# Dense matmuls behind a block of values issued as two of 64 stationary columns

## The chip, the cores and the metric

The kernel runs on one core of a Trainium2 chip, as one program. The metric is the device time of one execution in microseconds (us). A core has TensorE (PE: matmuls, with the loads of their stationary operand recorded apart as PEld), VectorE (DVE), ScalarE (ACT), GpSimd (POOL) and SyncE (SP), which run side by side and wait for each other through semaphores.

## What is computed

Sigmoid attention over 8 batches, 12 heads, 448 tokens and a head dimension of 64, and behind it a two-layer block with a gated hidden layer:

```python
scores = scale * np.matmul(q, k.transpose(0, 1, 3, 2)) - np.log(S)
attn = 1.0 / (1.0 + np.exp(-scores))
attn_out = np.matmul(attn, v)                         # (8, 12, 448, 64)
x = np.ascontiguousarray(attn_out.transpose(0, 2, 1, 3)).reshape(B * S, H * D)   # (3584, 768)
h = x @ w_in                                          # w_in: 768 x 2048
g = h * (1.0 / (1.0 + np.exp(-beta * h)))
out = (g @ w_out)                                     # w_out: 2048 x 768, out: float32
```

## The kernel before

All matmul operands are float16, sums are float32 in eight PSUM banks of 128 x 512. A matmul has a stationary operand (rows x columns, loaded first) and a moving one that streams past it; `128*64` in the profile means 128 rows and 64 columns of stationary operand. A matmul that uses fewer rows or columns than 128 is put at a `tile_position` in the array, and such matmuls can run beside each other at different positions.

The work on TensorE is of four kinds.

**Scores** (`score`, line 229). Heads are taken in pairs ("slots"), two slots are a quad, 24 quads in all, three for each batch. A *visit* (`visit`) computes the scores of one quad for one block of keys: eight matmuls of 32*128 over 448 queries (blocks 0 to 2 of 128 keys), or, for the last block of 64 keys, eight or, two quads at once, sixteen of 32*64. The scores of a visit fill the four score banks, and one ScalarE instruction turns them into weights (`weigh_two`, line 257, 1792 elements in each of 128 partitions), held in `attns`.

**Values** (`attend`, line 332). Once all four key blocks of a quad have weights, sixteen matmuls sum weights times values: four of 64*64 for the last block, then twelve of 128*64 in pairs, one head at column 0 and the other at column 64. VectorE copies the two sums to `xTs` (line 341).

**First layer** (`blocks`, line 523): for two batches at a time, 168 matmuls of 128*128 in one run, in a seven-product scheme, with sixteen dense units between them. Three such runs lie at 128.70, 215.97 and 302.53 us. The first two batches take the plain `dense1` (line 354) instead.

**Dense units.** Everything else, from 42 us on mostly the second layer (`strassen`, line 643, also a seven-product scheme on sums of two hidden tiles; `single`, line 437; `dense2`, line 384). A unit is one matmul, 128*128 over 384 columns in the second layer and over 448 in `dense1`. The units stand in a list, `fill`, in a fixed order; the eight units of one product add up in one bank, which is held from the product's first unit until VectorE or ScalarE may take it out.

The order of TensorE's work is written by a planner that runs when the kernel is built. From 42 us on it goes through 74 visits (n = 0 to 73). After the score matmuls of visit n it sets

```python
todo = left_us(L1B) if g < 2 * QPB else left_us(len(fill)) - RESERVE[n >= max(turn_at)]
pace = (todo + phase["values"] * AV_US) / phase["visits"]
owed = pace + MORE.get(n, 0) * M2_US
```

where `left_us` is the cost of the units left, 0.164 us each in the second layer (`M2_US`) and 0.148 in `dense1`; `phase` counts the visits and the blocks of values that are left until the next run of first-layer blocks; and `MORE` is a table of corrections by visit. Then units are issued while half a unit's cost is below `owed`, each taking its cost off. The values of a quad become due in the next quad's first visit. They are issued in the first place where `spent`, the units already issued in this visit, is at least `LATE.get(n, 0)` (3 at visit 8, 10 at visits 68 and 72, and at seven others), and take `AV_US` off `owed`. In a quad's first visit (`jt` is 0) they also need `clear()`: fewer than two banks held by dense sums, or two held and the next unit opening none (a product's third and fourth group and the first half of its fifth count as opening). In later visits of the quad, units are issued until `clear()` holds. After the last visit, and before visits 33 and 54, `first_layer` issues values that are due, the rest of the units but eight, and the run of blocks, which itself takes sixteen units.

Of the kernel before, what the change touches and what calls it, by code (L numbers as in the profile page):

```python
# [13 lines left out]
def kernel(  # L14
# [10 lines left out]
    nc = tc.nc  # L25
# [3 lines left out]
    B, H, S, D = q.shape  # L29
# [109 lines left out]
    def last_base(s: int) -> int:  # L139
        return (s % 2 ^ swapped(s // 2)) * KL  # L140
# [76 lines left out]
    def score_tile():  # L217
        i, j = scored[n_sc[0] % len(scored)]
        n_sc[0] += 1
        width[i] = width[j] = S  # L220
        return ps[:, i : j + 1]

    def score(sco, u0: int, s: int, jt: int, hh: int, e: int, c0: int, n: int):
        g, lo = s // 2, (s % 2 * 2 + hh) * BLK
        assert (g, "k") in ready and all(
            (g, "q", c) in ready for c in range(c0 // BLK, (c0 + n) // BLK, NB // 2)
        )
        base, nk = (last_base(s), KL) if jt == JF else (0, P)
        nc.tensor.matmul(  # L229
            sco[base : base + nk, hh, u0 : u0 + n],  # L230
            kT[g][lo : lo + BLK, jt * P : jt * P + nk, e],
            qT[g][lo : lo + BLK, c0 : c0 + n, e],
            start=(e == 0),
            stop=(e == PAIR - 1),
            tile_position=(lo, base),
        )

    places = {}

    def weigh(sco, n: int):  # L240
# [28 lines left out]
        nc.scalar.copy(out=dummy, in_=attns[:, slot, 0, 0:1])  # L269

    def visit(g: int, jt: int, also=()):
        if jt < JF:
            todo = [[s] for s in (2 * g, 2 * g + 1)]
        else:
            todo = [[2 * h, 2 * h + 1] for h in (g, *also)]
        todo = [(score_tile(), slots) for slots in todo]
        for e in range(PAIR):
            for sco, slots in todo:
                for s in slots:
                    for hh in range(2):  # L280
                        score(sco, 0, s, jt, hh, e, 0, S)
        if len(todo) == 2 and len(scored) == 2:
            ats = weigh_two(ps[:, 0:4, 0:S], places.get(g, ()))
        else:
            ats = [weigh(sco, S) for sco, _ in todo]
        for slot, (_, slots) in zip(ats if n_sc[0] % 2 == 0 or len(todo) == 1 else ats[::-1], todo):
            for s in slots:
                at_use(slot, (s, jt, 0), slice(0, S))
        return ats[-1]


    def half_visit(g: int, c0: int, second: int):
        slots = (2 * g, 2 * g + 1)
        scos = [score_tile() for _ in slots]
        plan = [(s, jt, sco, jt * QH) for jt in (0, 1) for s, sco in zip(slots, scos)]
        widths = [S, S]
        if second:
            plan = [(s, 2, sco, 0) for s, sco in zip(slots, scos)]
            plan += [(s, JF, scos[0], QH) for s in slots]
            widths = [S, QH]  # L300
        for i in range(0, len(plan), 2):
            for e in range(PAIR):
                for s, jt, sco, u0 in plan[i : i + 2]:
                    for hh in range(2):
                        score(sco, u0, s, jt, hh, e, c0, QH)
        if len(scored) == 2 and not second:
            two = weigh_two(ps[:, 0:4, 0:S], ())
            ats = dict(zip(map(id, scos), two if n_sc[0] % 2 == 0 else two[::-1]))
        else:
            ats = {id(sco): weigh(sco, n) for sco, n in zip(scos, widths)}  # L310
        for s, jt, sco, u0 in plan:
            at_use(ats[id(sco)], (s, jt, c0), slice(u0, u0 + QH))

    def attend(g: int, c0: int, n: int, part=(0, 1)):
        b, t = divmod(g, QPB)
        if b not in xTs:
            xTs[b] = xTp.tile([P, NHC, S], FP16, tag="xT", name="xT")
        assert (b, "v") in ready and (b, "full", t, HQ - 1) in ready
        slots = [2 * g + x for x in part]
        avs = [bank() for _ in slots]  # L320
        todo = [(s, av, jt) for s, av in zip(slots, avs) for jt in range(JF)]
        rest = [(s, av, JF) for s, av in zip(slots, avs)]
        todo = rest + todo if n == S else todo + rest
        first, last = {}, {}
        for s, _, jt in todo:
            first.setdefault(s, jt)
            last[s] = jt
        for s, av, jt in todo:
            at = at_take((s, jt, c0))
            base, nk = (last_base(s), KL) if jt == JF else (0, P)  # L330
            for hh in range(2):
                nc.tensor.matmul(  # L332
                    av[hh * D : (hh + 1) * D, 0:n],
                    vs[b][base : base + nk, 2 * (s % NPAIR) + hh, jt],
                    at[base : base + nk, hh, 0:n],
                    start=(jt == first[s]),
                    stop=(jt == last[s]),
                    tile_position=(base, hh * D),
                )
        for s, av in zip(slots, avs):  # L340
            nc.vector.tensor_copy(out=xTs[b][:, s % NPAIR, c0 : c0 + n], in_=av[:, 0:n])  # L341
            ready.update((b, s % NPAIR, c) for c in range(c0, c0 + n, QH))
# [4 lines left out]
    def dense1(b: int, dc: int, hc: int, c0: int = 0, n: int = S):  # L347

        off = (b % 2) * S + c0
        assert all((b, hc, c) in ready for c in range(c0, c0 + n, QH))  # L350
        if hc == 0:
            m2s[b, dc] = bank(n, (b, dc))
        m1 = m2s[b, dc]
        nc.tensor.matmul(  # L354
            m1,
            w_in16[:, hc, dc * P : (dc + 1) * P],
            xTs[b][:, hc, c0 : c0 + n],
            start=(hc == 0),
            stop=(hc == NHC - 1),
        )  # L360
        if hc < NHC - 1:
            return
        release((b, dc))
        assert "beta" in ready
        sg = sigp.tile([P, S], FP32, tag="sg", name="sg")
        nc.scalar.activation(  # L366
            out=sg[:, 0:n], in_=m1, func=AF.Sigmoid, bias=0.0, scale=beta_sb[:, dc : dc + 1]
        )
        nc.vector.tensor_tensor(  # L369
            out=gt[:, dc, off : off + n], in0=m1, in1=sg[:, 0:n], op=ALU.mult  # L370
        )
# [7 lines left out]
    def dense2(t: int, half: int, dc: int):  # L379

        if dc == 0:
            m2s[t, half] = bank(HALF, (t, half))
        m2 = m2s[t, half]
        nc.tensor.matmul(  # L384
            m2,
            gt[:, dc, cols(t)],
            w_out16[:, dc, half * HALF : (half + 1) * HALF],
            start=(dc == 0),
            stop=(dc == NDC - 1),
        )  # L390
        if dc == NDC - 1:
            leave(t, half, m2)
# [25 lines left out]
    def single(t: int, n: int, dc: int, piece=None):  # L418

        if (n, dc) == (0, 0):  # L420
            if (t, 0) not in sums:
                sum_of_halves(t)
            for half in range(1 + (t < NT - 1)):
                m2s[t, 1 - half] = bank(HALF, (t, 1 - half))
        if piece is not None and (n, dc) == (1, 0):
            m2s[t, 0, piece] = bank(CUTS[piece + 1] - CUTS[piece], (t, 0, piece))
        both = sums[t, 0]
        half, x, w = (
            (1, hid(t, 0), B12),
            (0, hid(t, 1), B21),  # L430
            (1, both, B22),
            (0, both, B11),
        )[n]
        m2 = m2s[(t, half) if piece is None else (t, half, piece)]
        stop = n > 1 and dc == ND - 1
        w = w[:, dc] if piece is None else w[:, dc, CUTS[piece] : CUTS[piece + 1]]
        nc.tensor.matmul(m2, x[:, dc], w, start=(n < 2 and dc == 0), stop=stop)  # L437
        if stop:
            leave(t, half, m2, piece)

# [99 lines left out]

    def blocks(b: int, other, scores: int):

        kept = {}
        rest = sorted(used, key=used.get)
        firsts = [i for i in rest if width[i] == S and i not in held.values()][:2]
# [17 lines left out]
        for i in range(NB1 + 1):  # L563
            p5 = scratch(6 + i % 2, 1).bitcast(FP32)
            if i < NB1:
# [6 lines left out]
                D = take("D", i)  # L572
# [59 lines left out]
    def strassen(t: int, i: int, dc: int):  # L632

        name, x, _, op, w = product(t, i)
# [5 lines left out]
        if first:  # L640
            m2s[t, name] = bank(HALF, (t, name))
        m2 = m2s[t, name]
        nc.tensor.matmul(  # L643
            m2,
            (x if op is None else sums[t, i])[:, dc],
            w[:, dc],
            start=first,
            stop=(dc == ND - 1),
# [108 lines left out]
    with tc.manual_schedule():  # L757
# [28 lines left out]
        for r, (to, n) in parts.items():  # L786
            nc.sync.dma_start(
                out=to[:, 0 : n * D],
# [96 lines left out]
        def left_us(n: int):  # L885
            return sum(u[0] for u in fill[at_fill[0] : n])

        AV_US = 1.5
        GLANCE = 3
        MORE = {  # L890
# [31 lines left out]
        def values(g: int):  # L922
# [3 lines left out]
            attend(g, 0, S)  # L926
            owed -= AV_US
            phase["values"] -= 1
# [15 lines left out]
        for n, (g, jt, also) in enumerate(visits):  # L944
# [25 lines left out]
            todo = left_us(L1B) if g < 2 * QPB else left_us(len(fill)) - RESERVE[n >= max(turn_at)]  # L970
            pace = (todo + phase["values"] * AV_US) / phase["visits"]
            phase["visits"] -= 1
# [46 lines left out]
```

## Time and profile before

| | |
|---|---|
| time, median of 3 runs | 373.27 us (373.2 to 373.52) |
| span of the profiled execution, first to last instruction | 371.2 us |
| time outside that span, by the median | 2.1 us |
| PE busy | 365.5 us (98%), 2906 matmuls |
| ACT busy | 259.7 us (70%) |
| DVE busy | 254.4 us (69%) |
| POOL busy | 80.5 us (22%) |
| visits 0 to 32, 33 to 53, 54 to 73, from their first score to the blocks' start | 86.58, 52.75 and 52.02 us |

The profile shows one execution. Its times are single ones and are compared with the median by adding the time outside the span. A busy TensorE isn't one at its peak, since the ends of matmuls are modelled; starts are measured, and what follows is read from differences of starts. Lines of the timeline merge equal instructions that follow each other: the first number is the start of the first, the second the length of all.

### The profile page before, as it was taken

What the parts mean: (1) busy time and instruction counts of PE and PEld (TensorE: products, weight loads), DVE (VectorE), ACT (ScalarE), POOL (GpSimd) and SP (SyncE); (2) the same over time, 40 slices, a digit from 0 to 9 for tenths busy, and PEclk for the clock granted to TensorE, in tenths of its full rate; (3) what the DMA queues carried; (4) which work ended last, traced back from release to release, by engine and by line L of the source; (5) the groups of instructions that cost most, each with busy time, mean ns of one, the idle gap of its engine ahead of it and who ended that gap; (6) DMA issues with size and microseconds to landing.
All of it is one profiled execution on the core that took longest, in us unless ns stands there. A gap on an engine that the chain in (4) does not pass through costs nothing.

```text
span 371.2 us, 7295 instructions
## 1 busy us (share of the span) xinstructions
PE 365.5 (98%) x2906; PEld 184.6 (50%) x2906; DVE 254.4 (69%) x479; ACT 259.7 (70%) x311; POOL 80.5 (22%) x120
## 2 busy tenths in 40 slices
PE   8999999999999999999999999999999999999997
PEld 4566544443444455544444445554444455555665
DVE  4435796777496967787666667778767667679671
ACT  5995766798967668887877749887678647883000
POOL 7732431221131013233131003233100002230000
PEclk9999999999999999999999999999999999999999
DMA  9999999893368030029829410017803111000334
GB/s 173 195 197 204 202 205 206 193 123 51 51 86 174 1 87 1 2 49 130 171 37 212 106 25 20 3 29 110 171 2 85 44 44 42 1 2 1 87 85 129
DMA packets 36226, 34.65 MB, mean 93 GB/s; under 512 B 9424, under 2 KB 32608, under 8 KB 36192
## 3 DMA queue, kind: packets, MB, share of 16 engines
q0 software_dynamic: 30288, 22.47, 42.3%
q1 hardware_dynamic: 5904, 11.71, 11.1%
q8 instruction: 23, 0.38, 0.4%
q14 instruction: 11, 0.09, 0.1%
HBM read 45.62 MB, written 11.01 MB: 153 GB/s over the span
## 4 chain that ended last, share of the span: by engine, by line
PE 93%; ACT 5%; issue 1%; DVE 0%; ACTq 0%
PE ps L643 27%; PE ps L523 26%; PE ps L229 11%; PE ps L332 10%; PE ps L354 9%; PE ps L384 4%; PE ps L437 4%; ACT attns L242 3%; ACT attns L257 1%; PE ps L812 1%; ACT sg L366 1%; DVE gt L369 0%; ACT osb L664 0%; DVE still L806 0%; ACT osb L399 0%
## 5 line engine op out<-in xcount | busy, mean ns | idle before, releaser
L257 ACT ACTIVATE attns<-ps,nlogs 128x1792 f16<-128x1792 f32 x75 | 131.7, 1756 | 41.1 <-PE ps L229 41.0
L643 PEld LDWEIGHTS <-sum 128*128 128x128 f16 x440 | 40.5, 98 | 37.3 <-issue 12.5
L537 POOL TENSOR_TENSOR gt<-attns,sg 128x448 f16<-128x448 f32 x21 | 23.9, 1137 | 141.7 <-ACT sg L534 141.7
L229 PE MATMUL ps<-qT,kT 32*128 32x448 f16 (+3 forms) x864 | 52.3, 339 | 1.1 <-ACT attns L242 0.6
L534 ACT ACTIVATE sg<-ps,beta_sb 128x448 f32<-128x448 f32 x72 | 45.2, 632 | 8.4 <-PE ps L523 5.9
L523 PE MATMUL ps<-xT,w_in 128*128 128x448 f16 x216 | 49.2, 353 | 0.0
L523 PE MATMUL ps<-xT,w_S 128*128 128x448 f16 x216 | 49.2, 352 | 0.0
L643 PE MATMUL ps<-w_T,sum 128*128 128x384 f16 x264 | 48.7, 327 | 0.0
L537 DVE TENSOR_TENSOR gt<-ps,sg 128x448 f16<-128x448 f32 x72 | 44.2, 618 | 4.0 <-ACT sg L534 3.8
L341 DVE CAST xT<-ps 128x448 f16<-128x448 f32 (+1 forms) x54 | 28.8, 567 | 21.5 <-PE ps L332 21.5
L523 PEld LDWEIGHTS <-w_in 128*128 128x128 f16 x288 | 28.0, 98 | 26.6 <-issue 0.7
L661 DVE TENSOR_TENSOR osb<-ps,osb 128x384 f32<-128x384 f32 x55 | 30.5, 554 | 15.1 <-PE ps L643 12.8
L332 PE MATMUL ps<-attns,v 128*64 128x448 f16 (+3 forms) x432 | 40.4, 340 | 0.1
L354 PE MATMUL ps<-xT,w_in 128*128 128x448 f16 (+1 forms) x240 | 39.5, 316 | 0.6 <-DVE gt L369 0.6
L630 DVE TENSOR_TENSOR sum<-gt 128x1024 f16<-128x1024 f16 x55 | 36.5, 678 | 0.2
L369 DVE TENSOR_TENSOR gt<-ps,sg 128x448 f16<-128x448 f32 (+1 forms) x40 | 20.0, 527 | 22.4 <-ACT sg L366 22.3
L125 POOL DMA_DIRECT2D raw<-in_q_dram x26 | 14.4, 555 | 92.8 <-DVE kT L212 84.7
L643 PE MATMUL ps<-w_out,gt 128*128 128x384 f16 x176 | 33.3, 327 | 0.0
L643 PE MATMUL ps<-w_out,sum 128*128 128x384 f16 x176 | 32.3, 327 | 0.0
L583 DVE TENSOR_TENSOR ps<-ps,attns 128x448 f32<-128x448 f32 x24 | 15.2, 632 | 23.3 <-PE ps L523 19.4
L523 PEld LDWEIGHTS <-w_S 128*128 128x128 f16 x216 | 21.1, 98 | 19.4
L354 PEld LDWEIGHTS <-w_in 128*128 128x128 f16 x240 | 22.0, 98 | 16.9 <-issue 5.8
(52 smaller groups left out, 364.3 us busy)
## 6 DMA issues: line engine op xcount, KB each, us to landing
out_dram<-osb SPq DMA_DIRECT2D x100, 96.0 KB, 2.2
raw<-in_k_dram POOLq DMA_DIRECT2D x23, 224.0 KB, 5.3
raw<-in_q_dram POOLq DMA_DIRECT2D x21, 224.0 KB, 4.1
v<-in_v_dram POOLq DMA_DIRECT2D x16, 192.0 KB, 6.9
w_in<-in_moe_w_in_dram POOLq DMA_DIRECT2D x8, 384.0 KB, 11.9
w_out<-in_moe_w_out_dram POOLq DMA_DIRECT2D x4, 768.0 KB, 15.0
v<-in_v_dram POOLq DMA_DIRECT2D x16, 144.0 KB, 7.5
out_dram<-osb SPq DMA_DIRECT2D x5, 144.0 KB, 2.4
```

The source lines that it names most:

```text
L229: nc.tensor.matmul(sco[base : base + nk, hh, u0 : u0 + n], kT[g][lo : lo + BLK, jt * P : jt * P + nk, e], qT[g][lo : lo + BLK, c0 : c0 + n ...
L257: nc.scalar.activation(out=attns[:, slot : slot + 2].rearrange("p n h s -> p (n h) s"), in_=sco, func=AF.Sigmoid, bias=nlogs[:, 0:1], scal ...
L332: nc.tensor.matmul(av[hh * D : (hh + 1) * D, 0:n], vs[b][base : base + nk, 2 * (s % NPAIR) + hh, jt], at[base : base + nk, hh, 0:n], start ...
L341: nc.vector.tensor_copy(out=xTs[b][:, s % NPAIR, c0 : c0 + n], in_=av[:, 0:n])
L354: nc.tensor.matmul(m1, w_in16[:, hc, dc * P : (dc + 1) * P], xTs[b][:, hc, c0 : c0 + n], start=(hc == 0), stop=(hc == NHC - 1),)
L369: nc.vector.tensor_tensor(out=gt[:, dc, off : off + n], in0=m1, in1=sg[:, 0:n], op=ALU.mult)
L523: nc.tensor.matmul(out, w[:, c, i * P : (i + 1) * P], m[:, c], start=(start and c == 0), stop=(c == KH - 1), skip_group_check=not start,)
L534: nc.scalar.activation(out=sg, in_=h, func=AF.Sigmoid, bias=0.0, scale=beta_sb[:, dc : dc + 1])
L537: return lambda: engine.tensor_tensor(out=gt[:, dc, b % 2 * S : b % 2 * S + S], in0=h, in1=sg, op=ALU.mult)
L630: nc.vector.tensor_tensor(out=sums[t, i], in0=x, in1=y, op=op)
L643: nc.tensor.matmul(m2, (x if op is None else sums[t, i])[:, dc], w[:, dc], start=first, stop=(dc == ND - 1), skip_group_check=i >= 4,)
L661: nc.vector.tensor_tensor(out=out, in0=in0, in1=in1, op=op)
```

## The change

A function `dense` takes the place of `nc.tensor.matmul` in the four functions that issue dense units (`dense1`, `dense2`, `single`, `strassen`). While `halves[0]` is set, it issues a unit as two matmuls with 64 stationary columns each, at column positions 0 and 64, with the same moving operand; each writes its half of the output's partitions. `halves[0]` is set behind every block of values over all 448 queries, and cleared by the next visit of scores and by the first-layer blocks. The planner's cost of a block of values, `AV_US`, goes from 1.5 to 1.4.

```diff
+    halves = [False]
+
+    def dense(out, w, x, **kw):
+
+        if not halves[0]:
+            nc.tensor.matmul(out, w, x, **kw)
+            return
+        for c in (0, D):
+            nc.tensor.matmul(out[c : c + D], w[:, c : c + D], x, tile_position=(0, c), **kw)
...
     def visit(g: int, jt: int, also=()):
+        halves[0] = False
...
     def half_visit(g: int, c0: int, second: int):
+        halves[0] = False
...
     def attend(g: int, c0: int, n: int, part=(0, 1)):
...
+        halves[0] = n == S
         for s, av in zip(slots, avs):
...
     def dense1(b: int, dc: int, hc: int, c0: int = 0, n: int = S):
...
-        nc.tensor.matmul(
+        dense(
             m1,
             w_in16[:, hc, dc * P : (dc + 1) * P],
...
     def dense2(t: int, half: int, dc: int):
...
-        nc.tensor.matmul(
+        dense(
...
     def single(t: int, n: int, dc: int, piece=None):
...
-        nc.tensor.matmul(m2, x[:, dc], w, start=(n < 2 and dc == 0), stop=stop)
+        dense(m2, x[:, dc], w, start=(n < 2 and dc == 0), stop=stop)
...
     def blocks(b: int, other, scores: int):
 
+        halves[0] = False
...
     def strassen(t: int, i: int, dc: int):
...
-        nc.tensor.matmul(
+        dense(
             m2,
...
-        AV_US = 1.5
+        AV_US = 1.4
```

## The prediction

> **What bounds the kernel now.** I read the page first, then the timeline of TensorE and ScalarE between 186 and 200 us, then TensorE's rows one by one where its work changes shape. From the page:
>
> ```profile
> span 371.2 us, 7295 instructions
> PE 365.5 (98%) x2906; PEld 184.6 (50%) x2906; DVE 254.4 (69%) x479; ACT 259.7 (70%) x311; POOL 80.5 (22%) x120
> ...
> PEclk9999999999999999999999999999999999999999
> ...
> PE 93%; ACT 5%; issue 1%; DVE 0%; ACTq 0%
> ```
>
> TensorE is busy all the time at full clock, and 93% of the chain that ended last is its own. The 5% of ScalarE in that chain are what the change can run into; the timeline shows where. Columns: start, length, engine, line, operation, count.
>
> ```profile
> 188.14 0.58 PE L229 MATMUL ps<-qT,kT 32*128 32x448 f16 x8
> 188.65 1.64 PE L332 MATMUL ps<-attns,v 64*64 64x448 f16 x16
> 190.22 0.34 PE L643 MATMUL ps<-w_T,sum 128*128 128x384 f16 x1
> 190.57 0.58 PE L229 MATMUL ps<-qT,kT 32*128 32x448 f16 x8
> ...
> 193.01 0.58 PE L229 MATMUL ps<-qT,kT 32*128 32x448 f16 x8
> 193.52 2.12 PE L643 MATMUL ps<-w_out,gt 128*128 128x384 f16 x12
> 195.57 0.57 PE L229 MATMUL ps<-qT,kT 32*128 32x448 f16 x8
> 196.08 1.64 PE L332 MATMUL ps<-attns,v 64*64 64x448 f16 x16
> 197.65 0.50 PE L643 MATMUL ps<-w_out,gt 128*128 128x384 f16 x2
> 198.08 0.57 PE L229 MATMUL ps<-qT,kT 32*128 32x448 f16 x8
> ```
> ```profile
> 193.63 1.75 ACT L257 ACTIVATE attns<-ps,nlogs 128x1792 f16<-128x1792 f32 x1 [0.68 <-PE ps L229]
> 196.20 1.75 ACT L257 ACTIVATE attns<-ps,nlogs 128x1792 f16<-128x1792 f32 x1 [0.81 <-PE ps L229]
> ```
>
> A visit goes score, perhaps values, then dense. The score matmuls need all four score banks, so a visit can't follow the one before until that one's sigmoid has ended: the sigmoid starts 0.62 us after the visit (193.01 to 193.63), takes 1.76, and the tightest next score starts 0.05 after its end. **No visit is shorter than 2.44 us.** TensorE's own time comes from differences of starts: score 0.51 until the next work (0.53 for a visit of 16), a dense unit of 384 columns 0.1625, of 448 0.189 (12 units of 384 and one change of shape take 195.57-193.52 = 2.05, so the change costs 0.10), values 1.57 with what follows them. So a visit with 12 dense units needs 2.55, with 11 needs 2.39 (and waits 0.05 for ScalarE), with values and two units 2.50, with values and one 2.33.
>
> What a change of shape costs, in a short window at the end of one block of values:
>
> ```profile
> 189.75 0.54 PE L332 MATMUL ps<-attns,v 128*64 128x448 f16 x4
> 190.22 0.34 PE L643 MATMUL ps<-w_T,sum 128*128 128x384 f16 x1
> ```
>
> Two pairs from 189.75 at 0.189 a pair would end at 190.13; the dense unit starts 0.097 later. Every change between 32, 64 and 128 rows or columns shows 0.09 to 0.12 in the single records of this trace; between matmuls of one shape it is nothing.
>
> **The change, part by part.**
>
> *Dense units in halves.* After values the dense unit becomes two matmuls of 64 columns side by side, the shape of the values' last twelve matmuls. Removed: the 0.097 between values and dense, wherever a score follows. Not removed: the change from dense to score. One block of values goes to a score directly (62.51 to 64.08 us) and shows 0.096 there, so leaving 64 columns costs what leaving 128 does. Added: one matmul and one load for each unit between values and score, 44 of them by the order below. The values' own pairs are the row for that: two matmuls of 448 columns start 3 ns apart and the next pair 189 ns later, exactly the step of one whole 128x128 matmul of 448. I price a pair at nothing. Its loads (109 ns each, from the groups by form, against 98 for a whole one) lie under the matmul before; if that cover were gone, 44 x 0.109 = 4.8 us. No other engine gains work or a wait: the result leaves the bank as before.
>
> *What the visits let through.* By the trace 16 blocks of values have dense units and then a score behind them. In the order of before, the next score comes 0.12 to 0.13 after the sigmoid's end in most of them (198.08 against 197.95 here), and 0.05 is the least, so of 0.097 some 0.06 to 0.075 arrives and the rest becomes a wait; visits with one unit get nothing.
>
> *AV_US from 1.5 to 1.4.* This moves dense units, and it is the larger part. Behind each visit the planner sets owed = (cost of the units left + AV_US x values left) / visits left, takes AV_US off at values, and issues units of 0.164 while owed is above 0.082. I worked this rule through from the kernel's text, unit by unit, with the banks that are held; with 1.5 it gives the trace's counts in all 74 visits. With 1.4 the pace falls (visit 57, the fourth after the second run of first-layer blocks: (22.632 + 6 x 1.5)/17 = 1.861 becomes 1.825), but after values more is left: 0.361 becomes 0.425, which buys 3 units and not 2. The same at visit 60.
>
> So at visit 67 (282.85 us) two units more have been issued, and there the rule tips. Values wait, in a visit's first key block, until at most two banks are held and the next unit opens none. In the order of before, the next unit at 67 is the last of a product's second group: two banks held, values go at once. One unit later a third bank opens; two units later it is open. The values of 67 go to visit 68, where LATE asks for ten units first; those of 71 go to 72 in the same way, behind 14 units; and for visit 73, the last, no dense unit is left. Units by visit, V for values, 67 to 73: before V1, 12, 12, 12, V2, 12, 14V; after 10, 10V, 10, 10, 9, 14V, V. The lengths:
>
> - Before: 2.44, 2.55, 2.55, 2.58, 2.50, 2.55, 4.45, in sum 19.62 (the trace: 282.85 to 302.53, 19.68).
> - After: visit 67 needs 2.23 and takes ScalarE's 2.43; 68 takes 0.51 + 1.63 + 0.10 + 1.57 = 3.80; 69 takes 2.43; 70 takes 2.48 (its sigmoid starts 0.67 after it); 71 takes 2.44 (own work 2.07); 72 takes 4.45.
> - Visit 73: its values need its own sigmoid. Two thirds of a microsecond of score and older values are done, then TensorE waits until 2.43, and the four remaining pairs take 0.87: 3.30. Before, 14 units lay there.
>
> After sums to 21.33, 1.71 more, for two units fewer.
>
> *The sum.* I carried both orders from visit to visit, each length the larger of TensorE's own and ScalarE's, with each visit's sigmoid start as measured; for the order of before this comes 0.6 us short of the trace over 260 us. Difference of the two: -0.32 at visit 33 (six gaps of 0.097, less waits of visits that now have 10 or 11 units), -0.52 at visit 54, -0.45 at visit 67 with two units ahead, then +1.71: **+1.26**. By parts: the halves alone -1.0 in the order of before, AV_US alone +2.3. First-layer blocks and the end have no half units and stay. The profiled execution has 371.2 us of span and some 2.1 around it, against a median of 373.27 in the three runs; the difference goes onto that: 374.5.
>
> **The rivals.**
>
> *Faster: the values stay at visit 67.* If the values of 67 and 71 were issued in their visits (no more than 643 of the units counted from visit 0 done there; I count 645), only the gains stay: 0.45 + two units ahead, 0.33, + 0.06 at visit 71: -0.84, 372.4. For it: the tipping hangs on one unit. Against: the rule gave all 74 counts of before, and with 1.4 it is the same text.
>
> *The gap is not one of shape.* If TensorE stops after values anyway (their sums end there and the operands are others), halves bring nothing: +2.3, 375.6. Against: in the values, one slot's sum follows another's without a gap.
>
> *The loads of a half unit lie open.* The row against it:
>
> ```profile
> 188.96 0.90 PEld L332 LDWEIGHTS <-v 128*64 128x64 f16 x12 [0.20 <-issue]
> ```
>
> Twelve loads of 109 ns, 1.31 us in series, lie in 0.90 us beside matmuls that keep their step. If they lay open all the same, each half unit would cost 0.109 more, 44 of them 4.8 us, and with the 1.26 of the sum it would be 379.3. The Trainium skill ("TensorE: Matmul & The Clock Gate", The mechanism) states that a load overlaps running matmuls only when its row group differs, and both halves use all rows. By that rule the time would be this rival's; the values' pairs, which also share their rows, speak against it.
>
> **How the numbers follow.** A measurement can tell about 0.2%, 0.75 us, from no change. My forecast, +1.26, has 0.64; its size is uncertain by 0.5 (sigmoid starts of 0.63 or 0.66 in all visits give +1.2 and +1.5; VectorE's leftover subtractions before the last blocks could add 0.2), so a tenth of it falls within 0.2%. The faster rival has 0.17, the gap that stays 0.12, the open loads 0.03, and 0.04 is left for waits that I don't see, on either side. Faster: 0.17 and half of the unseen, 0.19. Same: a tenth of my forecast, 0.07 with rounding. Slower: the rest, 0.74. The range leaves out the faster rival and the open loads, a fifth: from 373.3, a gain of the full 0.097 at 14 places (-1.36) with a cost of order at the small end, to 376.0, the gap that stays with sigmoids a little later.
>
> **What would show it.** Right: matmuls of 128*64 on lines that now call dense, 88 of them, and the first of them 0.19 after the last pair of values; scores of visits 36, 39, 46 and 50 starting 0.05 after the sigmoid's end; near 284 us ten dense units, then values, then a score; a gap of over 1 us in the last values before the third run of blocks. Wrong: one dense unit behind the values at 282 us, or 14 units ahead of the last values (the order is not what I worked out); 0.1 us still between values and half units; or a step of more than 0.17 from half unit to half unit.

## The result, and the profile after

The changed kernel takes 374.92 us (median of 5 runs, 374.86 to 375.21) against 373.27 (5 runs of before beside them): 1.0043 times as long, 95% interval 1.0031 to 1.0056. Forecast were 374.5 and a range of 373.3 to 376.0.

The page of after, the same lines as of before:

```profile
span 373.1 us, 7383 instructions
PE 365.0 (98%) x2950; PEld 187.0 (50%) x2950; DVE 254.5 (68%) x479; ACT 259.4 (70%) x311; POOL 80.8 (22%) x120
...
PEclk9999999999999999999999999999999999999999
...
PE 87%; ACT 8%; issue 2%; DMA 1%; DVE 1%; ACTq 0%
```

There are 44 matmuls and 44 loads more, the clock is the same, and ScalarE's share of the chain has gone from 5% to 8%: TensorE waits for it more. Where, the timeline of TensorE shows in two places. Lines have moved: scores are still L229, whole dense units L243, half units L246, values L344, the sigmoid L267, first-layer blocks L536. First the place that the prediction took as its example, visits 43 to 47 (the columns are start, length, engine, line, operation, count):

```profile
190.46 0.33 PE L246 MATMUL ps<-w_T,sum 128*64 128x384 f16 x2
190.91 0.58 PE L229 MATMUL ps<-qT,kT 32*128 32x448 f16 x8
...
195.90 0.58 PE L229 MATMUL ps<-qT,kT 32*128 32x448 f16 x8
196.41 1.64 PE L344 MATMUL ps<-attns,v 64*64 64x448 f16 x16
197.88 0.49 PE L246 MATMUL ps<-w_out,gt 128*64 128x384 f16 x4
198.33 0.58 PE L229 MATMUL ps<-qT,kT 32*128 32x448 f16 x8
```
```profile
196.53 1.75 ACT L267 ACTIVATE attns<-ps,nlogs 128x1792 f16<-128x1792 f32 x1 [0.81 <-PE ps L229]
```

Values to half units are 1.47 us (196.41 to 197.88) where values to whole units were 1.57: the gap is gone. Values, two units and the next score take 2.43 (195.90 to 198.33) where they took 2.51. The sigmoid, 196.53 to 198.28, sets that end now: the score starts 0.05 behind it, and with one unit (190.46 to 190.91, of which the unit and the change of shape are 0.26) TensorE idles for 0.19 before the score. Then the last visits. In before, the values of visit 67 have one unit behind them, and fourteen units lie ahead of the last values:

```profile
282.85 0.57 PE L229 MATMUL ps<-qT,kT 32*128 32x448 f16 x8
283.35 1.64 PE L332 MATMUL ps<-attns,v 64*64 64x448 f16 x16
284.92 0.34 PE L643 MATMUL ps<-w_out,gt 128*128 128x384 f16 x1
...
298.57 1.15 PE L437 MATMUL ps<-w_out,gt 128*128 128x384 f16 x6
299.56 1.46 PE L437 MATMUL ps<-w_out,sum 128*128 128x384 f16 x8
300.95 1.64 PE L332 MATMUL ps<-attns,v 64*64 64x448 f16 x16
302.53 1.31 PE L523 MATMUL ps<-xT,w_in 128*128 128x448 f16 x6
```

In after, visits 68, 71 and 73 look like this:

```profile
286.00 0.99 PE L243 MATMUL ps<-w_out,sum 128*128 128x384 f16 x5
286.82 0.98 PE L243 MATMUL ps<-w_T,sum 128*128 128x384 f16 x5
287.73 1.68 PE L344 MATMUL ps<-attns,v 64*64 64x448 f16 x16
...
294.24 0.58 PE L229 MATMUL ps<-qT,kT 32*128 32x448 f16 x8
294.75 1.64 PE L243 MATMUL ps<-w_out,gt 128*128 128x384 f16 x9
296.67 0.58 PE L229 MATMUL ps<-qT,kT 32*128 32x448 f16 x8 [0.28 <-ACT attns L267]
...
301.13 0.58 PE L229 MATMUL ps<-qT,kT 32*128 32x448 f16 x8
301.64 0.88 PE L344 MATMUL ps<-attns,v 64*64 64x448 f16 x8
303.57 0.95 PE L344 MATMUL ps<-attns,v 128*64 128x448 f16 x8 [1.04 <-ACT attns L267]
304.45 0.74 PE L536 MATMUL ps<-xT,w_in 128*128 128x448 f16 x3
```

Ten units stand ahead of the values of visit 68, nine units fill visit 71 (294.24 to 296.67, with a wait for the sigmoid), and behind the last visit no dense unit is left, so that the last values stop half way for 1.04 us until their own sigmoid has ended.

The first score of visit 0 starts at 42.12 us in before and at 42.42 in after, though the order is the same up to there; what differs is when the first loads land (a DMA of k is now 1% of the chain). So I count from that score:

| us from the first score of visit 0 to | before | after | difference | forecast |
|---|---|---|---|---|
| visit 33 | 121.10 | 121.31 | +0.21 | -0.32 |
| visit 54 | 208.39 | 208.29 | -0.10 | -0.52 |
| visit 67 | 240.73 | 240.64 | -0.09 | -0.45 |
| third run of blocks | 260.41 | 262.03 | +1.62 | +1.26 |
| start of the last matmul | 326.04 | 327.66 | +1.62 | +1.26 |

The order is the one that the prediction lists: the units of visits 67 to 73, three units at visits 57 and 60, and 44 half pairs in all. The last seven visits cost what was forecast, 1.71. One step is off, in the first stretch: the values of visit 18 stop for 0.6 us, in the middle of their four matmuls of 64*64. In before they run through, while VectorE (DVE) multiplies gates on line 369:

```profile
89.33 1.64 PE L332 MATMUL ps<-attns,v 64*64 64x448 f16 x16
90.90 0.74 PE L354 MATMUL ps<-xT,w_in 128*128 128x448 f16 x3
```
```profile
89.26 1.16 DVE L369 TENSOR_TENSOR gt<-ps,sg 128x448 f16<-128x448 f32 x2 [1.54 <-ACT sg L366]
```

In after, where that line is 382:

```profile
89.64 0.38 PE L344 MATMUL ps<-attns,v 64*64 64x448 f16 x2
90.25 1.63 PE L344 MATMUL ps<-attns,v 64*64 64x448 f16 x14 [0.23 <-DVE gt L382]
91.72 0.73 PE L246 MATMUL ps<-xT,w_in 128*64 128x448 f16 x6
```
```profile
89.57 1.16 DVE L382 TENSOR_TENSOR gt<-ps,sg 128x448 f16<-128x448 f32 x2 [1.54 <-ACT sg L379]
```

Two of the sixteen matmuls start, the other fourteen 0.61 later; the wait is for VectorE's gate multiplication (L382), which reads a first-layer sum out of a bank. The first of its two multiplications ends at 90.20, and the values go on at 90.25. VectorE isn't later than in before: in both the multiplication starts 0.44 us behind the score of visit 18.

### The profile page after: what moved, and what is told of

The parts are those of the page before. It is cut to its first block, busy times and chain, and to the rows that moved or that the text cites. A ratio compares the mean times of both kernels' runs of the same rounds, so it can differ in the third digit from the quotient of the medians.

```text
span 373.1 us, 7383 instructions
## 1 busy us (share of the span) xinstructions
PE 365.0 (98%) x2950; PEld 187.0 (50%) x2950; DVE 254.5 (68%) x479; ACT 259.4 (70%) x311; POOL 80.8 (22%) x120
## 4 chain that ended last, share of the span: by engine, by line
PE 87%; ACT 8%; issue 2%; DMA 1%; DVE 1%; ACTq 0%
PE ps L243 39%; PE ps L536 26%; PE ps L229 11%; PE ps L344 9%; ACT attns L267 4%; ACT attns L252 3%; PE ps L246 2%; ACT sg L379 1%; DMA gt<-in_k_dram 1%; DVE gt L382 0%; DVE kT L212 0%; ACT osb L678 0%; DVE raw L812 0%; DVE qT L200 0%; ACT osb L412 0%
## 5 line engine op out<-in xcount | busy, mean ns | idle before, releaser
L267 ACT ACTIVATE attns<-ps,nlogs 128x1792 f16<-128x1792 f32 x75 | 131.7, 1756 | 44.0 <-PE ps L229 43.8
L243 PEld LDWEIGHTS <-sum 128*128 128x128 f16 x478 | 44.3, 98 | 37.2 <-issue 9.6
L243 PE MATMUL ps<-w_out,gt 128*128 128x384 f16 (+2 forms) x312 | 56.2, 323 | 0.0
L229 PE MATMUL ps<-qT,kT 32*128 32x448 f16 (+3 forms) x864 | 52.3, 339 | 2.2 <-ACT attns L252 0.6
L536 PE MATMUL ps<-xT,w_in 128*128 128x448 f16 x216 | 49.2, 353 | 0.0
L536 PE MATMUL ps<-xT,w_S 128*128 128x448 f16 x216 | 49.2, 352 | 0.0
L243 PE MATMUL ps<-w_T,sum 128*128 128x384 f16 x246 | 44.4, 326 | 0.0
L344 PE MATMUL ps<-attns,v 128*64 128x448 f16 (+3 forms) x432 | 41.1, 340 | 1.3 <-ACT attns L267 1.0
L243 PE MATMUL ps<-w_out,sum 128*128 128x384 f16 (+2 forms) x232 | 41.8, 321 | 0.0
L536 PEld LDWEIGHTS <-w_in 128*128 128x128 f16 x288 | 27.9, 98 | 26.8 <-issue 1.0
L243 PEld LDWEIGHTS <-gt 128*128 128x128 f16 x312 | 28.5, 98 | 25.3 <-issue 8.1
L243 PE MATMUL ps<-xT,w_in 128*128 128x448 f16 (+1 forms) x230 | 37.1, 314 | 0.6 <-DVE gt L382 0.6
L382 DVE TENSOR_TENSOR gt<-ps,sg 128x448 f16<-128x448 f32 (+1 forms) x40 | 19.8, 527 | 22.6 <-ACT sg L379 22.5
L536 PEld LDWEIGHTS <-w_S 128*128 128x128 f16 x216 | 21.1, 98 | 19.4
```

The source lines that it names most:

```text
L229: nc.tensor.matmul(sco[base : base + nk, hh, u0 : u0 + n], kT[g][lo : lo + BLK, jt * P : jt * P + nk, e], qT[g][lo : lo + BLK, c0 : c0 + n ...
L243: nc.tensor.matmul(out, w, x, **kw)
L267: nc.scalar.activation(out=attns[:, slot : slot + 2].rearrange("p n h s -> p (n h) s"), in_=sco, func=AF.Sigmoid, bias=nlogs[:, 0:1], scal ...
L344: nc.tensor.matmul(av[hh * D : (hh + 1) * D, 0:n], vs[b][base : base + nk, 2 * (s % NPAIR) + hh, jt], at[base : base + nk, hh, 0:n], start ...
L382: nc.vector.tensor_tensor(out=gt[:, dc, off : off + n], in0=m1, in1=sg[:, 0:n], op=ALU.mult)
L536: nc.tensor.matmul(out, w[:, c, i * P : (i + 1) * P], m[:, c], start=(start and c == 0), stop=(c == KH - 1), skip_group_check=not start,)
```

## The experiments

Theory A is the prediction's: the gap between values and dense goes, a half pair costs what a whole unit costs, and the loss lies in the order that AV_US makes. The rival B is that the half units cost the time and the order is harmless. Times are medians; before had 373.28 beside the first four experiments (e1 to e4) and 373.32 beside the last three (e5 to e7).

**e1: half units without the new cost of values.**

```diff
-        AV_US = 1.4
+        AV_US = 1.5
```

> Dense units in halves behind values, but AV_US stays 1.5, so the order of the work is that of before. Theory A (each gap between values and dense, 0.097 us, goes; a half pair costs what a whole unit costs; the loss lies in the order): 1.0 us under before, about 372.3, with twelve or more of the 16 scores behind values 0.05 us after the end of the sigmoid. Rival B (the half units themselves cost: their second load and matmul lie open; the order is harmless): 1.5 us above before, about 374.9.

Measured 372.25 (5 runs), 0.9966 times before, interval 0.9953 to 0.9978. Faster by the forecast 1.0, and B falls. Twelve of the sixteen scores behind values start 0.05 us after the end of the sigmoid, the least that was expected. The last values have their fourteen units again, and no wait:

```profile
297.93 1.15 PE L243 MATMUL ps<-w_out,gt 128*128 128x384 f16 x6
298.92 1.46 PE L243 MATMUL ps<-w_out,sum 128*128 128x384 f16 x8
300.31 1.64 PE L344 MATMUL ps<-attns,v 64*64 64x448 f16 x16
301.88 1.31 PE L536 MATMUL ps<-xT,w_in 128*128 128x448 f16 x6
```

**e2: the new cost of values without half units.**

```diff
-        halves[0] = n == S
+        halves[0] = False
```

> AV_US 1.4 as in the change, but all dense units whole: the order of after without half units. Theory A: 1.1 us above after, about 376.0 (2.7 above before), with 0.097 us back between values and dense. Rival B (half units cost, order harmless): about before, 373.3.

Measured 376.21 (5 runs), 1.0072 times before (1.0059 to 1.0085). The order alone costs 2.9 us, 0.2 more than expected; its values of visit 18 stop for 0.60 us as in after. In its timeline the gap is back, 1.57 from values to dense:

```profile
197.01 1.64 PE L344 MATMUL ps<-attns,v 64*64 64x448 f16 x16
198.58 0.50 PE L243 MATMUL ps<-w_out,gt 128*128 128x384 f16 x2
```

**e3: two units fewer at visit 66**, which is all that the values of 67 and 71 need to stay in their visits:

```diff
-            54: 1, 59: 1, 62: 1, 67: -1,
+            54: 1, 59: 1, 62: 1, 66: -2, 67: -1,
```

> The change with one entry more in the table of corrections: two units fewer at visit 66, so that by the arithmetic of the planner the values of quads 21 and 22 are issued in visits 67 and 71 again and 15 dense units lie ahead of the last values. Theory A (1.7 us of the loss lie in visits 67 to 73): 1.75 us under after, about 373.2. Rival B (half units cost): as after, 374.9. Rival C (the loss is spread over all visits by a worse pace): under 0.3 us below after.

Measured 373.13 (11 runs), 0.9994 times before (0.9986 to 1.0003), 1.8 under after. Nothing else differs from after up to visit 66, and from visit 67 to the last matmul this kernel takes 85.30 us where after takes 87.02 and before 85.31. So the loss of the last visits is the order's, and lies there; C falls with B.

**e4: one unit fewer at visit 16**, so that the values of visit 18 come behind 306 units and not 307:

```diff
-            0: -1, 2: 1, 3: -4, 8: -3, 9: 1, 10: 1, 12: 2, 13: 1, 14: -2, 15: 1, 16: -1, 17: -2, 19: -1, 20: -2,
+            0: -1, 2: 1, 3: -4, 8: -3, 9: 1, 10: 1, 12: 2, 13: 1, 14: -2, 15: 1, 16: -2, 17: -2, 19: -1, 20: -2,
```

> The change with one unit fewer at visit 16, so that the values of visit 18 come after 306 units as in before and not after 307. Theory A (in after, the second sum of these values takes a bank whose first-layer sum VectorE hasn't read yet, because the unit more has opened another bank; that costs 0.6 us): 0.65 us under after, about 374.3, and no wait inside the values near 90 us. Rival D (VectorE is late there whatever the bank): as after, 374.9, with the wait still there.

Measured 374.39 (9 runs), 1.0028 times before (1.0018 to 1.0038), 0.5 under after; from visit 0 to visit 33 it takes 120.84 against 121.31. The unit comes back at visit 24; the rest of the order is that of after. The values run through:

```profile
89.43 0.58 PE L229 MATMUL ps<-qT,kT 32*128 32x448 f16 x8
89.94 1.64 PE L344 MATMUL ps<-attns,v 64*64 64x448 f16 x16
91.42 0.73 PE L246 MATMUL ps<-xT,w_in 128*64 128x448 f16 x6
```

With 306 units done no first-layer sum is open; with 307 a new one has just taken the bank that was free for longest, and the values' second sum gets the next, which VectorE hasn't read. That the wait goes with this one unit speaks for the bank and against D, and so does VectorE's own time: in e4 its multiplication starts 0.51 us behind the score of visit 18, no earlier than the 0.44 in after. Which bank it was is taken from the rule that allots them; the profile doesn't name banks.

**e5: all dense units of the visits in halves** (AV_US 1.5), against e1:

```diff
     def visit(g: int, jt: int, also=()):
-        halves[0] = False
+        halves[0] = True
```

> As e1 (halves, AV_US 1.5, the order of before), but every dense unit between visit 0 and the last blocks is issued as two halves, those inside the first-layer blocks excepted: 635 half pairs more than in e1. Theory A (a pair costs what one whole unit costs): as e1, 372.25, within 0.3. Rival (a pair's second load and matmul cost something that the 44 pairs were too few to show): 635 x 0.01 = 6 us above e1 for each 10 ns of price, less what the visits' waits for the sigmoid take up.

Measured 372.69 (11 runs), 0.9982 times before (0.9973 to 0.999): 0.44 above e1, outside the 0.3 of theory A and far under 10 ns a pair. From visit 0 to the last matmul it is 0.49. The single records say where: from half unit to half unit the step is 0.1625 at 384 columns and 0.189 at 448, as for whole units, but in 55 of the 56 places where half units follow another shape, the second pair comes 0.024 late (steps of 0.187 and 0.213; the exception is visit 27, where the first pair starts some 0.05 late already). Behind values that doesn't happen, since no shape changes there; the values' own second pair has paid it. Whole units in the same places have a smaller share of this: in e1 their second one comes 0.011 late (0.173 and 0.200). So halves add 0.013 there. The first half unit starts 0.004 sooner than a whole one, and the score behind the last one 0.003 later. That makes a visit that TensorE bounds 0.010 to 0.019 longer than in e1 and leaves one that the sigmoid bounds as it was; over all visits it sums to 0.50 us.

**e6: first-layer blocks and tail in halves too**, against e5:

```diff
     def single(t: int, n: int, dc: int, piece=None):
...
+        if piece is not None:
+            halves[0] = False
...
     def product1(b: int, i: int, n: int, out, start: bool):
...
-            nc.tensor.matmul(
+            dense(
...
     def blocks(b: int, other, scores: int):
-        halves[0] = False
```

> As e5, and the first-layer blocks and the dense units in and behind them in halves too, save the last tile's two narrow pieces: 1363 half pairs more than in e1, most of them in stretches where nothing but TensorE sets the time. Theory A: the three gaps between values and blocks go as well (3 x 0.097) and one change of shape is added in the last tile: 0.2 us under e1, about 372.05. Rival (a price per pair): 13.6 us above e1 for each 10 ns.

Measured 372.93 (11 runs, 372.26 to 373.46), 0.9986 times before (0.9977 to 0.9995), 0.7 above e1 and not 0.2 under it; e5's 0.44 is part of that. From visit 0 to the last matmul it is 0.08 above e5. Its second run of blocks, values included, takes 36.08 us where e5's takes 36.11: 0.03 under, though one gap of 0.097 is gone. The 184 pairs there have cost 0.07 us together, 0.4 ns each. The first run shows the same 0.03 (37.22 against 37.25). That is the price of a pair, and for the change's 44 it is nothing.

**e7: other corrections from visit 34 on**, against e1:

```diff
-            25: -2, 27: -1, 28: -1, 32: -1, 34: 1, 35: 1, 43: -1, 45: 1, 47: 1, 49: 1, 51: 1, 52: 2, 53: -1,
-            54: 1, 59: 1, 62: 1, 67: -1,
+            25: -2, 27: -1, 28: -1, 32: -1, 35: 1, 36: 1, 41: 1, 43: -1, 45: 1, 47: 1, 48: 1, 49: 1, 50: 1, 51: 1, 52: 2, 53: -1,
+            59: 1, 60: 1, 62: 1, 69: 1, 70: 1, 71: 1, 72: 1,
```

> As e1, with other entries in the table of corrections from visit 34 on (34, 54 and 67 dropped; 36, 41, 48, 50, 60, 69, 70, 71 and 72 raised by one), which by the arithmetic of the planner leaves fewer visits under the 2.44 us that the sigmoid needs. By theory A the lengths of the visits sum to 0.33 us less than in e1: about 371.9, the lowest of all. Rival (moving single units runs into waits that the arithmetic doesn't hold, for banks or VectorE): e1 or worse.

Measured 371.94 (5 runs, 371.87 to 372.16), 0.9962 times before (0.9948 to 0.9975), the lowest median. But against e1 it is inconclusive: from visit 0 to the last matmul the two profiles are 324.77 and 324.83 us, 0.06 apart where 0.33 was expected, and visit 0 began 0.36 earlier in this one, which no correction from visit 34 on can have done. So the median's closeness to the forecast doesn't bear out the arithmetic. Between visits 33 and 54 both take 86.96 us. Either kernel beats before and after; which of them is the better stays open.

## Why the prediction was right, and where it was not

**Direction and size.** Slower was forecast by 1.26 and measured as 1.65 by the medians, 1.62 between the same two points of the two traces.

**What bounds.** That no visit is shorter than 2.44 us held: visits 36, 39, 46 and 50 end 0.05 behind the sigmoid, as written. Of 0.097 a visit with two units gained 0.07 to 0.08, a visit with one nothing.

**Dense units in halves.** From the last pair of values to the first half unit the records show 0.189, so the whole gap went, in all 15 places where half units follow values. Alone (e1) this gives -1.0 by the medians, as forecast, and -1.21 from visit 0 to the last matmul. The gain in TensorE's own time is a little more than the gap of the prediction: behind values the second whole unit came 0.011 late as well (0.173 at 384 columns in before), and the second half unit doesn't (0.1625). Visits 15, 18 and 22, with three units each, are 0.10 to 0.11 shorter in e1 than in before. The price of a pair, taken as nothing, is 0.4 ns. The rival of loads that lie open is refuted by that, and with it, for this shape, the sentence that stood beside it: the Trainium skill ("TensorE: Matmul & The Clock Gate", The mechanism) has loads overlap running matmuls only where the row group differs, while here both halves use all rows and the step doesn't grow. The rival of a gap that isn't one of shape is refuted by after and e2, which have the same order: 1.47 us from values to dense with halves and 1.57 without.

**AV_US.** The tipping at visit 67 came as worked out, and with it the 1.71 us of the last seven visits (19.68 us before, 21.39 after). It isn't a sum that came out by chance: visits 67 to 73 took 2.43, 3.85, 2.43, 2.47, 2.43, 4.46 and 3.31, where 2.43, 3.80, 2.43, 2.48, 2.44, 4.45 and 3.30 were written. The prediction put AV_US alone at +2.3; e2 has +2.9, with the wait of visit 18 in it. The faster rival needed no more than 643 units there; e3 is that rival made true, and it loses those 1.7 us again. It ends at before's time and not 0.8 under it, since the wait of visit 18 and a visit with nine units remain.

**The step that failed** is the term of the first stretch: -0.32 was forecast up to visit 33, and +0.21 measured. For the halves the prediction held that no other engine gains a wait, since results leave the banks as before; that stands. Of the new order it asked how many banks are held, which decides when values are issued, but not which bank the values then get. At visit 18 they get one that VectorE is still to read: 0.61 us by the trace, 0.5 when it is taken away (e4), and then the stretch is at -0.27, near the forecast. It left "waits that I don't see" with a chance of 0.04, and this was one. The other stretches were a little better than forecast (-0.31 for -0.20 from visit 33 to 54, +0.01 for +0.07 from there to 67), so that 0.36 of the sum was missed. The miss of the sum is smaller than that of its first term because these two happened to go the other way.

## What to carry to other kernels

A gap where the matmul's shape changes can be closed by giving the next matmuls the shape of those before, as long as what follows isn't held by another engine: read what the next waiting instruction waits for before counting the gain. A cost constant in a planner is a change of the whole order; work the new order out unit by unit, and look at the end of each stretch, where the work that used to cover a wait may have run out. Follow not only how many buffers are taken but which one comes next, and who has still to read it.

## What the runs showed of the hardware

- A change of shape among 32*128, 64*64, 128*64 and 128*128, wherever one occurs here without a wait, costs 0.09 to 0.12 us between starts. A change into 128*64 makes the second pair 0.024 late as well, and one into 128*128 the second matmul 0.011. A change from values to half units, both 128*64, costs nothing.
- Two matmuls of 64 columns at positions 0 and 64 step like one of 128: 0.1625 us at 384 columns and 0.189 at 448, with 0.4 ns more a pair over long stretches.
- With the same order of work up to there, the first score of visit 0 starts between 42.10 and 42.79 us in the nine profiles. That is 0.7 us of spread from the start alone, as much as some of the effects here, so stretches of two traces are better compared from a point inside.
